# Windowed attention with a gated feed-forward on one core: scores and values as one whole-array product per query block, queries laid with zeros

## The chip, the cores and the metric

The kernel runs on one core of a Trainium2 chip. The metric is the device time of one execution in microseconds (us). The kernel before was timed three times: 671.68, 670.58 and 668.12 us, median 670.58. Inputs and outputs lie in device memory. The host lays the inputs out once, before the launch, and that is not timed.

## What is computed

There are four batches, eight heads, 768 positions and 64 features a head. Each position attends to the keys at a distance under 16, and to 24 summaries: the elementwise maximum of each block of 32 keys, with the mean of the same 32 values. The result of all heads side by side (3072 tokens of 512) goes through a feed-forward of width 2048 with a gate.

```python
k_sum = k.reshape(B, H, nb, 32, D).max(axis=3)
v_sum = v.reshape(B, H, nb, 32, D).mean(axis=3)
mask_l = np.abs(pos[:, None] - pos[None, :]) < 16
scores_l = np.where(mask_l, scale * q @ k.T, -1e9)
scores_s = scale * q @ k_sum.T + np.log(32)
a = softmax(concatenate([scores_l, scores_s]))
x = a @ concatenate([v, v_sum])
h = x @ w_in
g = np.where(h >= 1, h, np.where(h <= -1, 0.0, (h + 1) ** 2 / 4))
out = g @ w_out
```

## The kernel before

**Tiling.** A chunk is half a batch: 384 positions, six query blocks of 64. There are eight chunks (c), and in each four pairs of heads (p). A query block sees 96 neighbouring keys and 24 summaries, 120 columns. The partitions of a pair's tiles hold the 64 features of its first head, then those of its second.

**Attention of one pair.** Steps are named by a letter, chunk and pair; the letters are those of the table `steps` in the code. r, k, q, y and v load raw keys, windowed keys, queries, raw values and windowed values. R reduces raw keys to their maxima (DVE, tile ks), C copies them behind the windowed keys (POOL). Y, Z, V and W do the same for values, through a transpose on PE (tile vs_ps). S are the scores: for each of six blocks and each head one product of 64 features by 64 queries by 120 keys, into two tiles of PSUM (s_ps, one for each head). The two blocks of a step t go to partitions 0 to 63 and 64 to 127. M scales and masks (DVE, tile e) and finds the maxima (den). E is exp with its sum on ACT, D the reciprocal on DVE, N the norm on POOL. T transposes the weights on PE (t_ps), P copies them out of PSUM (ACT, tile pt). A are the values: for each block and head one product with 64 columns of v held and 64 columns of pt streamed, all into one PSUM tile o_ps. X copies o_ps to a rounded high part (ACT, xhi), and L subtracts it to get the low part (DVE, xlo).

**Feed-forward.** A chunk runs 16 steps f. F is the first product (tile h, 12 products of 384 columns: four head pairs, three of high and low parts each). G, H, I and J are the gate on ACT and DVE, O its low part on POOL. B is the second product, two steps behind F, into three PSUM tiles acc that live for the whole chunk (9 products of 512 columns). U and o copy a chunk's result out and store it. The weights are fetched (w) and split into high and low parts (a to e, on ACT, DVE and POOL) once, during chunk 0.

**Order.** The text OPENING lists chunk 0, and the attention of chunk 1, step by step for all engines. After it, the loop at the end of the function fixes the order on PE alone, and a scheduler places the work of the other engines and the DMA issues on SP's queue. In the loop, f = 0, 4, 8 and 12 of chunk c first run `meet`: the values of one pair of the next chunk (at f = 0: the fourth pair of this chunk), then at once the scores of the pair after it. f = 3, 7, 11 and 15 run `turn`: transposes of that pair, ahead of B.

**Buffers.** Six PSUM tiles are shared by scores, transposes, values and acc (pool `ps`), two are for h. Queries have four buffers (Q_BUFS), windowed keys three, windowed values two. Raw keys, raw values and results share three. Queries lie in device memory as blocks of 128 rows (both heads' features) by 128 columns, each head's 64 queries in its own half of the columns and zeros in the other half. Chunk 0 loads whole blocks; later chunks load the two parts that are not zero.

Of the kernel before, what the change touches and what calls it, by code (L numbers as in the profile page):

```python
# [19 lines left out]
P = 128  # L20
# [3 lines left out]
QB = 64  # L24
# [13 lines left out]
Q_BUFS = 4  # L38
# [10 lines left out]
F060 F061 F062 F063 F052 F053 J03 O03 B03 J04 O04 B04 e6 q12 q13 w9 wa wb wc a9 aa wd we wf c7 d7 e7 c8 d8 b9 ba bb  # L49
# [5 lines left out]
W11 V10 W10 S10 B0e M10 E101 D101 N101 E100 D100 N100 B0f U02 U00 S11 M11 E111 E110 S12 o02 U01 o01 T101 P101 D111  # L55
# [5 lines left out]
         [("kraw", 3), ("vraw", 3)], [("v", 2), ("v", 3)], [("q", 0), ("q", 1)]]  # L61
K_COPY = "vgvg"
# [4 lines left out]
def fused_kernel(ctx: ExitStack, tc: tile.TileContext, q2, kT, kwin, vT, vwin, w_in, w_out, mask, ident, out):  # L67
# [12 lines left out]
    mask_sb = const.tile([P, NT + 1, KA], F32, name="mask_sb")  # L80
# [94 lines left out]
    def load_queries(c, p):  # L175
        b, hf = divmod(c, NHALF)
        blocks = q2[b, p, :, hf * NB:(hf + 1) * NB, :]
        halves_of = [slice(j * D, (j + 1) * D) for j in range(2)]
        if c == 0:
            q_t = at_first["q", p]  # L180
            nc.sync.dma_start(out=q_t, in_=blocks)
            q_ts[c, p] = [q_t[rows, :, rows] for rows in halves_of]
        else:

            q_t = input_tile(load, "q", [P, NB, QB], c, p)
            for rows in halves_of:
                nc.sync.dma_start(out=q_t[rows], in_=blocks[rows, :, rows])
            q_ts[c, p] = [q_t[rows] for rows in halves_of]
# [43 lines left out]
    def scores(c, p):  # L232


        q_t, k_t = q_ts[c, p], k_ts[c, p]
        s_ps = [ps.tile([P, 512], F32, tag="ps", name=f"s_ps{c}_{p}_{j}") for j in range(2)]
        for t in range(NT):
            for j in range(2):
                rows = slice(j * D, (j + 1) * D)
                for i in range(2):  # L240
                    blk = 2 * t + i
                    nc.tensor.matmul(s_ps[j][i * QB:(i + 1) * QB, t * KA:(t + 1) * KA],  # L242
                                     q_t[j][:, blk], k_t[rows, blk, :], start=True, stop=True)
# [37 lines left out]
    def values(c, p):  # L281
        o_pss[c, p] = ps.tile([P, 512], F32, tag="ps", name=f"o_ps{c}_{p}")
        for blk in range(NB):
            cols = slice(blk * QB, (blk + 1) * QB)
            for j in range(2):
                nc.tensor.matmul(o_pss[c, p][j * D:(j + 1) * D, cols], v_ts[c, p][:KA, blk, j * D:(j + 1) * D],  # L286
                                 pts[c, p, j][:KA, cols], start=True, stop=True)

    def high(c, p):
        hi = xpool.tile([P, T], F32R, tag=f"xhi{p}", name=f"xhi{c}_{p}")  # L290
        lo = xpool.tile([P, T], F32R, tag=f"xlo{p}", name=f"xlo{c}_{p}")
        nc.scalar.copy(out=hi, in_=o_pss[c, p][:, :T])  # L292
        xs[c, p] = (hi, lo)

    def low(c, p):
        hi, lo = xs[c, p]
        nc.vector.tensor_tensor(out=lo, in0=o_pss[c, p][:, :T], in1=hi.bitcast(F32), op=ALU.subtract)  # L297
# [188 lines left out]
```

## Time and profile before

| | us |
|---|---|
| median of three runs | 670.58 |
| the profiled execution, its span | 670.7 |
| PE busy (matmul) | 633.5 |
| PE busy (weight load) | 559.4 |
| ACT busy | 367.5 |
| POOL busy | 267.1 |
| DVE busy | 259.4 |
| mean granted TensorE clock | 0.982 |

The profiler's span runs from the first to the last instruction. PE is matmul, PEld the load of the operand that is held in the array, DVE the vector engine, ACT the scalar engine, POOL the general engine, SP the queue that issues the DMAs. "x12" is a number of instructions, "idle before" the idle time of the engine just before them with what ended it. The ends of matmul records are modelled, so that records which follow each other overlap by the time that the array takes to drain; starts are what to read.

### The profile page before, as it was taken

The numbers are of one execution on the slowest core, as the hardware profiler recorded it, in microseconds if no ns is written. First come the engines' busy times: TensorE is split into PE (matmuls) and PEld (weight loads), VectorE is DVE, ScalarE is ACT, GpSimd is POOL, SyncE is SP. The second block draws the span as 40 slices with busy tenths as digits, with TensorE's granted clock in tenths as the row PEclk, the third lists the DMA queues.
The fourth block names the chain that finished last, engine by engine and source line by source line (L and its number), as shares of the span: only waits on it lengthen the run. The fifth ranks groups of instructions, "written<-read, shape, count | busy, mean of one in ns | idle before, by whom it ended". The sixth has DMA issues, their size and how long they took to land.

```text
span 670.7 us, 11802 instructions
## 1 busy us (share of the span) xinstructions
PE 633.5 (94%) x4448; PEld 559.4 (83%) x4448; DVE 259.4 (39%) x561; ACT 367.5 (55%) x945; POOL 267.1 (40%) x300
## 2 busy tenths in 40 slices
PE   2579998779999999999999999999999999999997
PEld 2478986668888888988888889888888988889996
DVE  5899974642233321245322322336222322311111
ACT  3889745555555545555554554555545645544332
POOL 2589996333332333234333333334233333322221
PEclk9789999879999999999999999999999999999999
DMA  8999703851111401154111311135110200000001
GB/s 285 311 354 323 250 1 85 248 145 52 53 52 53 145 19 35 52 169 124 53 53 48 106 45 52 52 112 181 53 42 11 88 19 19 1 17 32 1 1 47
DMA packets 49768, 63.56 MB, mean 95 GB/s; under 512 B 24880, under 2 KB 33328, under 8 KB 49712
## 3 DMA queue, kind: packets, MB, share of 16 engines
q1 hardware_dynamic: 49712, 62.81, 30.9%
q8 instruction: 35, 0.57, 0.4%
q14 instruction: 21, 0.17, 0.1%
HBM read 56.51 MB, written 6.29 MB: 94 GB/s over the span
## 4 chain that ended last, share of the span: by engine, by line
PE 82%; DMA 7%; ACT 4%; DVE 4%; issue 2%; POOL 1%; SPq 0%; ACTq 0%; DVEq 0%; POOLq 0%
PE h L307 36%; PE acc L338 36%; PE o_ps L286 4%; PE s_ps L242 3%; DMA raw<-in_w_out 3%; PE t_ps L275 3%; DMA raw<-in_w_in 2%; DMA kraw<-in_kT 1%; ACT e L260 1%; DMA first<-in_vT 1%; DMA first<-in_kT 1%; ACT raw L110 1%; DVE c L124 1%; DVE w L130 1%; DVE c L127 1%
## 5 line engine op out<-in xcount | busy, mean ns | idle before, releaser
L307 PE MATMUL h<-xhi,halves 128*128 128x384 f32 x1024 | 285.4, 341 | 5.6 <-DVE t L319 5.5
L338 PE MATMUL acc<-halves,ghi 128*128 128x512 f32 x768 | 240.2, 394 | 0.0
L329 POOL TENSOR_TENSOR glo<-t,ghi 128x384 fp32r<-128x384 f32 x128 | 129.3, 1013 | 200.6 <-ACT ghi L324 194.5
L307 PEld LDWEIGHTS h<-xhi,halves 128*128 128x128 f32 x1024 | 188.5, 189 | 14.1 <-DVE t L319 4.8
L319 DVE SCALAR_TENSOR_TENSOR t<-h,t 128x384 f32<-128x384 f32 x128 | 70.8, 557 | 280.7 <-ACT t L316 268.9
L307 PE MATMUL h<-xlo,halves 128*128 128x384 f32 x512 | 173.3, 338 | 0.0
L338 PEld LDWEIGHTS acc<-halves,ghi 128*128 128x128 f32 x768 | 145.1, 189 | 27.9
L338 PE MATMUL acc<-halves,glo 128*128 128x512 f32 x384 | 154.2, 401 | 0.0
L313 ACT ACTIVATE t<-h,ones_half 128x384 f32<-128x384 f32 x128 | 73.6, 578 | 130.5 <-PE h L307 120.0
L260 ACT ACTIVATE e<-e,den 128x120 f32<-128x120 f32 x192 | 73.3, 383 | 63.8 <-DVE den L255 63.8
L324 ACT CAST ghi<-t 128x384 fp32r<-128x384 f32 x128 | 65.3, 513 | 64.5 <-DVE t L319 64.0
L307 PEld LDWEIGHTS h<-xlo,halves 128*128 128x128 f32 x512 | 96.8, 189 | 4.3 <-DVE xlo L297 0.4
L338 PEld LDWEIGHTS acc<-halves,glo 128*128 128x128 f32 x384 | 72.5, 189 | 12.3 <-issue 1.0
L270 POOL TENSOR_TENSOR e<-e,den 128x360 f32<-128x360 f32 x64 | 49.8, 790 | 61.6 <-DVE den L266 55.8
L316 ACT ACTIVATE t<-t 128x384 f32<-128x384 f32 x128 | 66.8, 525 | 3.7
L214 POOL COPY k<-ks 128x144 f32<-128x144 f32 x30 | 9.2, 310 | 86.4 <-DMA k<-in_kwin 61.1
L143 POOL TENSOR_TENSOR halves<-w,halves 128x1024 fp32r<-128x1024 f32 x16 | 38.6, 2415 | 0.9
L230 POOL COPY v<-v 24x640 f32<-24x640 f32 x30 | 21.5, 717 | 39.7 <-issue 37.2
L286 PEld LDWEIGHTS o_ps<-pt,v 120*64 120x64 f32 x720 | 25.0, 144 | 13.8 <-ACT ghi L324 7.5
L297 DVE TENSOR_TENSOR xlo<-o_ps,xhi 128x384 fp32r<-128x384 f32 x32 | 17.7, 554 | 47.3 <-ACT xhi L292 47.3
L260 ACT ACTIVATION_READ_ACCUMULATOR e<-e,den 128x1 f32 x192 | 35.9, 187 | 0.0
L275 PE MATMUL t_ps<-ident_sb,e 128*120 128x128 f32 x192 | 30.8, 298 | 5.2 <-POOL e L270 5.0
(56 smaller groups left out, 426.4 us busy)
## 6 DMA issues: line engine op xcount, KB each, us to landing
k<-in_kwin SPq DMA_DIRECT2D x28, 360.0 KB, 4.3
v<-in_vwin SPq DMA_DIRECT2D x30, 288.0 KB, 3.1
raw<-in_w_in SPq DMA_DIRECT2D x16, 512.0 KB, 10.8
raw<-in_w_out SPq DMA_DIRECT2D x16, 512.0 KB, 11.0
out<-o SPq DMA_DIRECT2D x24, 256.0 KB, 2.1
q<-in_q SPq DMA_DIRECT2D x56, 96.0 KB, 4.0
kraw<-in_kT SPq DMA_DIRECT2D x13, 384.0 KB, 3.8
vraw<-in_vT SPq DMA_DIRECT2D x13, 384.0 KB, 3.8
```

The lines of the kernel that those rows point to most:

```text
L143: nc.gpsimd.tensor_tensor(out=lo, in0=converting[i].bitcast(F32), in1=hi.bitcast(F32), op=ALU.subtract)
L260: nc.scalar.activation(out=e[:, t, :], in_=e[:, t, :], func=AF.Exp, bias=nm[:, t:t + 1], scale=1.0, accum_out=den[:, t:t + 1])
L270: nc.gpsimd.tensor_tensor(out=e, in0=e, in1=den.unsqueeze(2).broadcast_to([P, NT, KA]), op=ALU.mult)
L275: nc.tensor.transpose(t_pss[c, p, j][:KA, t * P:(t + 1) * P], es[c, p, j][:, t, :], ident_sb)
L286: nc.tensor.matmul(o_pss[c, p][j * D:(j + 1) * D, cols], v_ts[c, p][:KA, blk, j * D:(j + 1) * D], pts[c, p, j][:KA, cols], start=True, sto ...
L307: nc.tensor.matmul(hs[c, f][:, :T], weight["win", f][w][:, k * P:(k + 1) * P], x, start=(k == 0 and n == 0), stop=(k == NK - 1 and n == 2))
L313: nc.scalar.activation(out=ts[c, f], in_=hs[c, f][:, :T], func=AF.Relu, bias=ones_half, scale=0.5)
L316: nc.scalar.square(out=ts[c, f], in_=ts[c, f])
L319: nc.vector.scalar_tensor_tensor(out=ts[c, f], in0=hs[c, f][:, :T], scalar=1.0, in1=ts[c, f], op0=ALU.max, op1=ALU.min)
L324: nc.scalar.copy(out=hi, in_=ts[c, f])
L329: nc.gpsimd.tensor_tensor(out=lo, in0=ts[c, f], in1=hi.bitcast(F32), op=ALU.subtract)
L338: nc.tensor.matmul(acc[c][i], a[:, rows], weight["wout", f][w], start=(f == 0 and n == 0), stop=(f == NF - 1 and n == 2))
```

## The change

- **Queries** are loaded as whole blocks, zeros included, in every chunk: one DMA of 384 KB for a pair in place of two of 96 KB. Q_BUFS goes from 4 to 2. In OPENING the loads of queries 2 and 3 of chunk 1 (q12, q13) move to behind the scores S10 and S11.
- **Scores**: one product per block for both heads, 128 rows by 128 held columns by 120 streamed ones; the zeros keep the heads apart. A row of s_ps is now a query of the first head (0 to 63) or of the second, and the two tiles hold blocks 0 to 2 and 3 to 5. The mask tile has five positions instead of four, loaded by one DMA, and the second tile uses them one further on.
- **Values**, from chunk 2 on: one product per block with all 128 columns of v held and 128 columns of pt streamed, into two PSUM tiles of three blocks. Half of the results (one head's weights with the other head's values) is not used. X and L read the used quarters: four instructions of 64 partitions by 192 columns each, in place of one of 128 by 384. Chunks 0 and 1 (`QUARTERED`) keep twelve products into one tile.
- **Order in the loop**: `meet` is split. Scores stay ahead of F; values follow F of the same step (at f = 0 they stay first).

```diff
-Q_BUFS = 4
+Q_BUFS = 2
+QUARTERED = (0, 1)
...
-    mask_sb = const.tile([P, NT + 1, KA], F32, name="mask_sb")
+    mask_sb = const.tile([P, 2 * NT - 1, KA], F32, name="mask_sb")
...
-            q_t = input_tile(load, "q", [P, NB, QB], c, p)
-            for rows in halves_of:
-                nc.sync.dma_start(out=q_t[rows], in_=blocks[rows, :, rows])
-            q_ts[c, p] = [q_t[rows] for rows in halves_of]
+        q_ts[c, p] = input_tile(load, "q", [P, NB, P], c, p)
+        nc.sync.dma_start(out=q_ts[c, p], in_=q2[b, p, :, hf * NB:(hf + 1) * NB, :])
...
-        for t in range(NT):
-            for j in range(2):
-                rows = slice(j * D, (j + 1) * D)
-                for i in range(2):
-                    blk = 2 * t + i
-                    nc.tensor.matmul(s_ps[j][i * QB:(i + 1) * QB, t * KA:(t + 1) * KA],
-                                     q_t[j][:, blk], k_t[rows, blk, :], start=True, stop=True)
+        for blk in range(NB):
+            j, t = divmod(blk, NT)
+            nc.tensor.matmul(s_ps[j][:, t * KA:(t + 1) * KA], q_ts[c, p][:, blk, :], k_ts[c, p][:, blk, :], start=True, stop=True)
...
+            for g in range(2):
+                o_ps = ps.tile([P, 512], F32, tag="ps", name=f"o_ps{c}_{p}_{g}")
+                for t in range(NT):
+                    cols = slice(t * P, (t + 1) * P)
+                    nc.tensor.matmul(o_ps[:, cols], v_t[:KA, g * NT + t, :], pts[c, p, g][:KA, cols], start=True, stop=True)
+                for j in range(2):
+                    rows = slice(j * D, (j + 1) * D)
+                    own = o_ps[rows, :T].rearrange("p (t h q) -> p t h q", h=2, q=QB)[:, :, j, :]
+                    o_pss[c, p].append((rows, slice(g * NT * QB, (g + 1) * NT * QB), own))
...
-        nc.scalar.copy(out=hi, in_=o_pss[c, p][:, :T])
+        for rows, cols, o in o_pss[c, p]:
+            nc.scalar.copy(out=hi[rows, cols] if c in QUARTERED else shaped(hi[rows, cols]), in_=o)
...
-        nc.vector.tensor_tensor(out=lo, in0=o_pss[c, p][:, :T], in1=hi.bitcast(F32), op=ALU.subtract)
+        for rows, cols, o in o_pss[c, p]:
+            hi, lo = (x[rows, cols] if c in QUARTERED else shaped(x[rows, cols]) for x in xs[c, p])
+            nc.vector.tensor_tensor(out=lo, in0=o, in1=hi.bitcast(F32), op=ALU.subtract)
...
-                if f % 4 == 0:
-                    meet(c, NPAIR - 1) if f == 0 else meet(c + 1, f // 4 - 1)
-                    if f == 0:
-                        do(f"B{c - 1}{NF - LAG:x}")
+                pair, at = divmod(f, NF // NPAIR)
+                if f == 0:
+                    valued(c, NPAIR - 1)
+                    do(f"B{c - 1}{NF - LAG:x}")
+                if at == 0:
+                    scored(c + 1, pair)
                 s = f"{c}{f:x}"
                 do(f"F{s}0 F{s}1 F{s}2 F{s}3 G{s} H{s} I{s} J{s} O{s}")
-                if f % 4 == 3 and c + 1 < NCH:
-                    turn(c + 1, f // 4)
+                if at == 0 and pair:
+                    valued(c + 1, pair - 1)
+                if at == 3 and c + 1 < NCH:
+                    turn(c + 1, pair)
```

On PE, in chunk 2 at f = 4, these rows stood behind the acc products of f = 1. The digits behind a name are chunk and pair (and head or half), the last number a running one; "x2" is two products in a row.

```order
L338 MATMUL acc2_2_2422<-halves2_557,ghi2_1_2395 128x512 x2
L286 MATMUL o_ps3_0_2484<-pt3_0_0_2461,v3_0_2328 64x64
L286 MATMUL o_ps3_0_2484<-pt3_0_1_2467,v3_0_2328 64x64
L242 MATMUL s_ps3_1_0_2501<-k3_1_2469,q3_1_2471 64x120 x2
L242 MATMUL s_ps3_1_1_2502<-k3_1_2469,q3_1_2471 64x120 x2
L307 MATMUL h2_4_2537<-xhi2_0_1685,halves3_564 128x384
```

The two o_ps rows stand six times in turn, the two s_ps rows three times. In the same place of the changed program:

```order
L341 MATMUL acc2_2_2338<-halves2_532,ghi2_1_2311 128x512 x2
L227 MATMUL s_ps3_1_0_2399<-k3_1_2385,q3_1_2387 128x120 x3
L227 MATMUL s_ps3_1_1_2400<-k3_1_2385,q3_1_2387 128x120 x3
L310 MATMUL h2_4_2429<-xhi2_0_1674,halves3_539 128x384
L310 MATMUL h2_4_2429<-xhi2_3_2206,halves3_539 128x384
L281 MATMUL o_ps3_0_0_2450<-pt3_0_0_2377,v3_0_2253 128x128 x3
L281 MATMUL o_ps3_0_1_2454<-pt3_0_1_2383,v3_0_2253 128x128 x3
L341 MATMUL acc2_0_2336<-halves3_539,glo2_2_2333 128x512
```

Of the twelve h products between scores and values the first and the last are shown. Twelve and twelve products became six and six, and the values moved behind h.

On DVE, where chunk 1 takes over from chunk 0, the reciprocals of chunk 1's third and fourth pair (den1_2, den1_3) stood among the reductions of batch 2's raw keys and values (ks2, vs2):

```order
L265 TENSOR_SCALAR den1_2_1_1326<-den1_2_1_1326 128x3
L218 TENSOR_REDUCE vs2_0_1559<-vraw2_0_1555 128x24
L266 RECIPROCAL den1_2_1_1326<-den1_2_1_1326 128x3
L265 TENSOR_SCALAR den1_3_0_1381<-den1_3_0_1381 128x3
L211 TENSOR_REDUCE ks2_1_1660<-kraw2_1_1653 128x24
L266 RECIPROCAL den1_3_0_1381<-den1_3_0_1381 128x3
L266 RECIPROCAL den1_3_1_1383<-den1_3_1_1383 128x3
```

Now:

```order
L249 TENSOR_SCALAR den1_2_1_1279<-den1_2_1_1279 128x3
L202 TENSOR_REDUCE ks2_0_1464<-kraw2_0_1458 128x24
L250 RECIPROCAL den1_2_1_1279<-den1_2_1_1279 128x3
L249 TENSOR_SCALAR den1_3_0_1328<-den1_3_0_1328 128x3
L209 TENSOR_REDUCE vs2_0_1499<-vraw2_0_1495 128x24
L250 RECIPROCAL den1_3_0_1328<-den1_3_0_1328 128x3
L250 RECIPROCAL den1_3_1_1330<-den1_3_1_1330 128x3
L202 TENSOR_REDUCE ks2_1_1599<-kraw2_1_1593 128x24
```

The reduction of the second pair's keys (ks2_1) moved behind the last reciprocals; that of the third pair moved behind the masks of chunk 2's first scores, ahead of the gates that follow.

On SP's queue, the loads between the last weights of chunk 0 and the first raw keys of batch 2 stood so:

```order
L173 DMA k1_3_1183<-in_kwin 128x720
L187 DMA q2_0_1515<-in_q2 64x6x64 x2
L350 DMA out<-o0_2_1251 128x512
L173 DMA k2_0_1513<-in_kwin 128x720
L187 DMA q2_1_1657<-in_q2 64x6x64
L167 DMA kraw2_0_1511<-in_kT 128x768
```

Now:

```order
L174 DMA k1_3_1150<-in_kwin 128x720
L179 DMA q1_2_1174<-in_q2 128x768
L179 DMA q1_3_1226<-in_q2 128x768
L353 DMA out<-o0_2_1214 128x512
L174 DMA k2_0_1460<-in_kwin 128x720
L353 DMA out<-o0_1_1251 128x512
L353 DMA out<-o0_0_1216 128x512
L168 DMA kraw2_0_1458<-in_kT 128x768
L188 DMA v1_2_1342<-in_vwin 96x768
```

Two query loads of chunk 1 stand ahead of the first result's store, and the queries of chunk 2 moved behind the raw keys.

More of the change, by code (lines that the diff above doesn't have):

```diff
@@ L48 @@
 c4 d4 e4 b6 b7 b8 I02 J02 F040 F041 F042 F043 O02 B02 a7 a8 c5 c6 d5 e5 d6 q10 q11 G03 H03 I03 F050 F051 G04 H04 I04
-F060 F061 F062 F063 F052 F053 J03 O03 B03 J04 O04 B04 e6 q12 q13 w9 wa wb wc a9 aa wd we wf c7 d7 e7 c8 d8 b9 ba bb
+F060 F061 F062 F063 F052 F053 J03 O03 B03 J04 O04 B04 e6 w9 wa wb wc a9 aa wd we wf c7 d7 e7 c8 d8 b9 ba bb
 G05 G06 H06 I06 F070 F071 F072 F073 H05 I05 J05 F080 J06 O05 F081 F082 F083 O06 B05 G07 H07 e8 c9 d9 I07 J07 O07 F090
@@ L54 @@
 O0d B0d k10 k11 k12 v10 v11 bf cf df ef G0e H0e I0e G0f H0f I0f J0e J0f O0e O0f k13 C10 C11 C12 C13 Z10 Z11 V11 Z12
-W11 V10 W10 S10 B0e M10 E101 D101 N101 E100 D100 N100 B0f U02 U00 S11 M11 E111 E110 S12 o02 U01 o01 T101 P101 D111
+W11 V10 W10 S10 q12 B0e M10 E101 D101 N101 E100 D100 N100 B0f U02 U00 S11 q13 M11 E111 E110 S12 o02 U01 o01 T101 P101 D111
 N111 o00 D110 N110 T100 P100 M12 S13 E120 D120 N120 A10 X10 L10 T111 P111 T110 P110 M13 E121 D121 N121 F100 v12 V12
@@ L176, in load_queries @@
         b, hf = divmod(c, NHALF)
[L177 to L183, printed above, removed]
-            q_t = input_tile(load, "q", [P, NB, QB], c, p)
-            for rows in halves_of:
-                nc.sync.dma_start(out=q_t[rows], in_=blocks[rows, :, rows])
-            q_ts[c, p] = [q_t[rows] for rows in halves_of]
+        q_ts[c, p] = input_tile(load, "q", [P, NB, P], c, p)
+        nc.sync.dma_start(out=q_ts[c, p], in_=q2[b, p, :, hf * NB:(hf + 1) * NB, :])
     def load_raw_vals(c, p):
@@ L281, in values, with shaped @@
     def values(c, p):
[L282 to L287, printed above, removed]
+        v_t = v_ts[c, p]
+        if c in QUARTERED:
+            o_ps = ps.tile([P, 512], F32, tag="ps", name=f"o_ps{c}_{p}")
+            for blk in range(NB):
+                g, t = divmod(blk, NT)
+                for j in range(2):
+                    nc.tensor.matmul(o_ps[j * D:(j + 1) * D, blk * QB:(blk + 1) * QB], v_t[:KA, blk, j * D:(j + 1) * D],
+                                     pts[c, p, g][:KA, t * P + j * D:t * P + (j + 1) * D], start=True, stop=True)
+            o_pss[c, p] = [(slice(0, P), slice(0, T), o_ps[:, :T])]
+        else:
+            o_pss[c, p] = []
+            for g in range(2):
[3 more added lines that the diff above has]
+                    nc.tensor.matmul(o_ps[:, cols], v_t[:KA, g * NT + t, :], pts[c, p, g][:KA, cols], start=True, stop=True)
+                for j in range(2):
+                    rows = slice(j * D, (j + 1) * D)
+                    own = o_ps[rows, :T].rearrange("p (t h q) -> p t h q", h=2, q=QB)[:, :, j, :]
+                    o_pss[c, p].append((rows, slice(g * NT * QB, (g + 1) * NT * QB), own))
+    def shaped(ap):
+        return ap.rearrange("p (t q) -> p t q", q=QB)
     def high(c, p):
@@ L353, in load_constants @@
     def load_constants():
-        for i in range(2):
-            rows = slice(i * QB, (i + 1) * QB)
-            nc.sync.dma_start(out=mask_sb[rows], in_=mask[rows, i:i + NT + 1])
+        nc.sync.dma_start(out=mask_sb, in_=mask)
         nc.sync.dma_start(out=ident_sb, in_=ident)
@@ L380, in heads, with follow, valued, scored @@
                 (f"y{s} " if first else "") + f"v{s} " + (f"Y{s} " if first else ""))
-    def meet(c, p):
+    def follow(c, p):
+        return (c, p + 1) if p + 1 < NPAIR else (c + 1, 0)
+    def valued(c, p):
         if c < NCH:
             do(f"A{c}{p} X{c}{p} L{c}{p}")
-        c, p = (c, p + 1) if p + 1 < NPAIR else (c + 1, 0)
+    def scored(c, p):
         if c < NCH:
-            before, scored, valued = heads(c, p)
-            do(before + " " + scored + " " + valued)
+            do(" ".join(heads(c, p)))
     def turn(c, p):
@@ L394, in turn @@
         do(f"Z{s} V{s} W{s} T{s}0 P{s}0 T{s}1 P{s}1")
-        c, p = (c, p + 1) if p + 1 < NPAIR else (c + 1, 0)
+        c, p = follow(c, p)
         if c < NCH:
```

4 lines of the change are left out of this document (1 added, 3 removed).

## The prediction

> **What bounds the kernel now.** The page first: how full TensorE (PE) is, over the span and in 40 slices of it, and the chain that ended last.
>
> ```profile
> PE 633.5 (94%) x4448; PEld 559.4 (83%) x4448; DVE 259.4 (39%) x561; ACT 367.5 (55%) x945; POOL 267.1 (40%) x300
> PE   2579998779999999999999999999999999999997
> PE 82%; DMA 7%; ACT 4%; DVE 4%; issue 2%; POOL 1%; SPq 0%; ACTq 0%; DVEq 0%; POOLq 0%
> ```
>
> PE carries 82% of the chain. Next the windows, to see whether it ever rests in the steady part:
>
> ```profile
> 150.00:250.00 100.00, 100.00 (x754) 88.60 (x753) 29.63 (x70) 54.17 (x148) 34.46 (x42) 1.00 0.21 60
> 450.00:550.00 100.00, 100.00 (x718) 89.32 (x717) 33.10 (x73) 53.81 (x146) 34.97 (x44) 1.00 0.24 74
> ```
>
> The columns are PE, weight load (PEld), DVE, ACT, POOL, clock, DMA share. From 150 on PE is never without an instruction and at full clock; ACT is half idle, DVE two thirds. There, time added to or taken from PE goes one to one into the end. A full PE may still drain between shapes, so I read its timeline in one place where values and scores stand together (start, length from first start to last end):
>
> ```profile
> 302.86 0.33 PE L307 MATMUL h<-xhi,halves 128*128 128x384 f32 x1
> 303.03 0.27 PE L222 MATMUL vs_ps<-ident_sb,vs 128*24 128x128 f32 x1
> 303.14 0.82 PE L275 MATMUL t_ps<-ident_sb,e 128*120 128x128 f32 x6
> ...
> 304.02 0.62 PE L338 MATMUL acc<-halves,ghi 128*128 128x512 f32 x2
> ...
> 305.17 0.39 PE L338 MATMUL acc<-halves,glo 128*128 128x512 f32 x1
> 305.40 0.62 PE L338 MATMUL acc<-halves,ghi 128*128 128x512 f32 x2
> 305.95 0.92 PE L286 MATMUL o_ps<-pt,v 120*64 120x64 f32 x24
> 306.80 0.85 PE L242 MATMUL s_ps<-k,q 64*64 64x120 f32 x24
> 307.57 0.45 PE L307 MATMUL h<-xhi,halves 128*128 128x384 f32 x1
> 307.86 0.34 PE L307 MATMUL h<-xlo,halves 128*128 128x384 f32 x1
> 308.03 0.51 PE L307 MATMUL h<-xhi,halves 128*128 128x384 f32 x2
> ```
>
> A 512-column product starts 0.23 after the one before it (305.17, 305.40), a 384-column one 0.17 (307.86, 308.03). The last acc product thus starts at 305.63 and has streamed by 305.86. The first h product counts as starting one step ahead of the second, at 307.69. **Values and scores together cost 307.69 − 305.86 = 1.83**: values 0.85 (to about 306.70), scores 0.98.
>
> **What runs at once inside.** Twelve products stand as 24 records: two records to a product. A narrow window of the scores shows their beat:
>
> ```profile
> 307.16 0.49 PE L242 MATMUL s_ps<-k,q 64*64 64x120 f32 x12
> ...
> L242 PE MATMUL s_ps<-k,q x672: 262/263/314, 106.7 to 577.0; 64*64 64x120 f32 x168
> L286 PE MATMUL o_ps<-pt,v x720: 222/222/370, 20.0 to 595.7; 120*64 120x64 f32 x180
> ```
>
> The twelve, 0.26 each, start within 0.49 − 0.26 = 0.23. That is three groups of four, about 0.10 apart: four quarter-array records (64 rows by 64 columns) stream their 120 columns at the same time. Six groups are 0.62; the other 0.36 of the 0.98 goes at the two edges of the burst. Values: the last of 24 starts 0.92 − 0.22 = 0.70 after the first, 11 steps of 0.06 for pairs of half-array records.
>
> **The change on PE.** Six products use the whole array instead of twelve that share it: 12 records that cannot share. No row has a full-array fp32 product of this kind. Its nearest row in streaming is the transpose: six start within 0.82 − 0.27 = 0.55, a step of 0.11 for 128 columns; a score group gives 0.10 for 120. The other limit is the weight load, now 128 columns instead of 64:
>
> ```profile
> 303.69 0.19 PEld L338 LDWEIGHTS acc<-halves,glo 128*128 128x128 f32 x1
> ...
> 307.57 0.19 PEld L307 LDWEIGHTS h<-xhi,halves 128*128 128x128 f32 x1 [0.16 <-issue]
> 307.68 0.19 PEld L307 LDWEIGHTS h<-xlo,halves 128*128 128x128 f32 x1
> ```
>
> The load of 303.69 lets its acc product begin in effect at 304.02 − 0.23 = 303.79, and that of 307.57 its h product at 307.69: 0.10 to 0.12 from load to stream. Load and stream give the same 0.11, so I take **0.11 a record**. Below, 0.10 (scores all stream, load hidden); above, 0.19, if no load ran beside a stream.
>
> The Trainium skill, "TensorE: Matmul & The Clock Gate", section "LDWEIGHTS (loading the stationary operand)", has the load go with its columns, P / 1.2 ns. By it 128 columns are 107 ns, above the 0.10 of the scores' stream, so twelve score records would be 1.28 rather than 1.23. The row of 303.69 bears that out.
>
> Values: 12 × 0.11 = 1.32, against 0.85: +0.47. Scores: 1.32 against 0.98: +0.34. The edges go: vs_ps after h (302.86, 303.03) keeps the plain step of 0.17, so full-array products of other types follow without a drain. The sum is +0.81 where both stand together. That is 23 places: three in chunk 1's loop, four in each of chunks 2 to 6; the last values, in chunk 7, stand alone:
>
> ```profile
> 594.40 0.62 PE L338 MATMUL acc<-halves,ghi 128*128 128x512 f32 x2
> 594.96 0.92 PE L286 MATMUL o_ps<-pt,v 120*64 120x64 f32 x24
> 595.80 0.50 PE L338 MATMUL acc<-halves,glo 128*128 128x512 f32 x1
> 596.14 0.63 PE L338 MATMUL acc<-halves,ghi 128*128 128x512 f32 x2
> ```
>
> These cost 596.14 − 0.23 − 594.86 = 1.05, now 1.32: +0.27. **Steady part: 23 × 0.81 + 0.27 = 18.9.** At 0.10 a score record it is 16.1.
>
> **The copies out of PSUM.** One copy and one subtraction per pair become four each, of 64x192, from chunk 2 on.
>
> ```profile
> L292 ACT CAST xhi<-o_ps 128x384 fp32r<-128x384 f32 x32 | 15.2, 477 | 25.2 <-PE o_ps L286 25.0
> L226 ACT ACTIVATE v<-vs_ps 24x128 f32<-24x128 f32 x30 | 7.8, 264 | 2.5 <-PE vs_ps L222 1.8
> L297 DVE TENSOR_TENSOR xlo<-o_ps,xhi 128x384 fp32r<-128x384 f32 x32 | 17.7, 554 | 47.3 <-ACT xhi L292 47.3
> ```
>
> A 192-column copy lies between 0.26 and 0.48; I take 0.33, and 0.36 for the subtraction: +0.8 on ACT and +0.9 on DVE in 19 us, on engines with 45% and two thirds free. Only the fourth pair is needed soon: its values stand at the head of a chunk, and h wants it after one acc step (2.07), the scores (1.32) and nine h products (1.56), 4.9 later. Four copies and the last subtraction take about 1.8, at most 2.6. Cost nothing; if that cover were gone, six chunks would pay what is late. Exps and gates behind the extra copies on ACT are late by under 1 us, and their products two h steps away (over 4 us).
>
> **The opening.** The four score bursts of chunk 0 run at the low clock:
>
> ```profile
> 9.57 1.48 PE L242 MATMUL s_ps<-k,first 64*64 64x120 f32 x24 [9.57 <-POOL first L214]
> 36.84 1.54 PE L275 MATMUL t_ps<-ident_sb,e 128*120 128x128 f32 x6
> 25.25 1.10 ACT L110 ACTIVATE raw<-raw 128x1024 f32<-128x1024 f32 x1 [1.17 <-DMA raw<-in_w_in]
> 17.04 0.42 PE L222 MATMUL vs_ps<-ident_sb,vs 128*24 128x128 f32 x1
> 40.56 11.42 SPq L187 DMA_DIRECT2D q<-in_q  x8
> 48.00:106.00 58.00, 57.77 (x289) 51.24 (x287) 49.06 (x85) 42.63 (x64) 57.36 (x40) 1.00 0.57 175
> ```
>
> Transposes there step by 0.22 (1.54 less the 0.42 of one, over five), so a burst is 12 × 0.22 = 2.6 instead of about 1.3: +1.3 four times, 5.2. The first values stand behind all four, and ACT copies them ahead of its first weight (L110), for which it waits 1.17. Above, 5.2 − 1.17 = 4.0 reaches the weight conversions, which then keep POOL full; below, nothing. I take **+1.1**, nearer to nothing, because the second and third slice have PE busy 5 and 7 tenths: the bursts slide into gaps.
>
> The queries of chunk 1: eight loads held the queue for 11.42; now two whole-block loads go there and two later, so at most those 11 us go. But from 48 to 106 POOL is busy for 57.36 of 58.00 and PE for 57.77: earlier weights find both full. I take 0; if DMA were the limit there, it would be up to −11.
>
> **From chunk 0 to chunk 1** (106 to 140) PE waits:
>
> ```profile
> 126.55 0.54 PE L275 MATMUL t_ps<-ident_sb,e 128*120 128x128 f32 x3 [2.50 <-POOL e L270]
> 130.27 0.55 PE L275 MATMUL t_ps<-ident_sb,e 128*120 128x128 f32 x3 [1.15 <-POOL e L270]
> 139.72 0.69 PE L307 MATMUL h<-xhi,halves 128*128 128x384 f32 x1 [3.94 <-DVE t L319]
> ...
> 128.09 0.95 DVE L211 TENSOR_REDUCE ks<-kraw 128x24 f32<-128x768 f32 x1 [1.57 <-DMA kraw<-in_kT]
> ...
> k<-in_kwin SPq DMA_DIRECT2D x28, 360.0 KB, 4.3
> ```
>
> Five score bursts here (chunk 1's four, chunk 2's first) add 5 × 0.34 = 1.7. Two stalls may shrink: the key reduction of the next batch no longer stands ahead of the last reciprocals on DVE. What is late next is the 3.94: on DVE the third pair's key reduction now stands ahead of the gates that free h, its load behind v on the SP queue, which waits for the fourth pair's values. With two query buffers the third pair's queries of chunk 1 load only after its first scores, some 5 us ahead of their use, about what the landing of such a load takes (4.3 for 360 KB); out, kraw and vraw are queued behind them. In sum 0, between −4 and +4.
>
> **Sum.** 670.7 (the profiled span, the median of the runs to 0.1) + 18.9 + 1.1 + 0 = **690.7**.
>
> **Rivals.**
> *Faster: each record has a fixed price.* 48 records in 1.83 are 0.038 each; with 24 fewer the place costs 0.92: 23 × −0.9 = −21, **650**. It decides below 1.83 / 24 = 0.076 a record. For it: the averages 0.035 and 0.041 of the two bursts are near each other. Against it: four records start inside one 0.10 beat, and transposes step by 0.11. 3%.
> The Trainium skill, "TensorEngine Tiling", section "Instruction Overhead", states about 60 cycles of overhead for each matmul. If that were the price here, halving the records would pay as in this rival; the groups of four speak against it.
> *Loads don't hide behind full-array fp32 streams:* 0.19 a record, 2.3 a burst, 23 × 2.7 + 1.2 = 63: **735**. The transposes' step of 0.11 speaks against it. 4%.
> *A new PSUM wait:* values now take two slots, of three beside acc, while two hold scores; the second frees when DVE's mask has read. The mask has twelve h products (12 × 0.17 = 2.1) for it; a reduction of 0.95 in its way in the twelve pairs that load new keys is 12 × 0.95 = 11: **702**. 8%.
> *The waits of the transition go:* 2.50, 1.15 and 3.94 are 7.6, less the 1.7 of the scores' growth that they hid: **685**; with the loads of the opening on the path as well, **675**. 4%.
>
> **How the numbers follow.** 80% for the forecast, 1% for no measurable change by something not listed. 684 to 699 comes from the bounds (−2.8 for the stream and −4; +4, +3 and 1 for a wait now and then); it leaves out the two far rivals, the PSUM wait and the 675. A measurement tells about 0.5% (3.4 us) from no change: faster by over 0.5% 3%, within it 1%, slower 96%.
>
> **What would show it.** s_ps and o_ps at six products (12 records) each, starting 0.11 apart, 1.3 a burst; the period of four f steps grows from 19.2 to 20.0; no PE wait from 150 to 600; q gone from 40 to 52. I am wrong if the records start under 0.08 or over 0.13 apart, if PE waits for DVE ahead of the second half of o_ps, or if chunk 2 begins more than 5 us from where it did.

## The result and the profile after

The changed kernel takes 689.92 us (median of 4 runs, 688.76 to 692.42); the kernel before, on the same chip, 671.13 (668.12 to 673.95). The ratio is 1.0285, interval [1.0245, 1.0325]: slower. The profiled execution spans 688.4 us, against 670.7. The forecast was 690.7, from 684 to 699.

The page first: the line of busy times, PE's 40 slices, and the shares of the chain that ended last.

```profile
PE 653.2 (95%) x3776; PEld 594.7 (86%) x3776; DVE 285.0 (41%) x633; ACT 381.9 (55%) x1017; POOL 267.8 (39%) x300
PE   4489998789999999999999999999999999999997
PE 88%; ACT 3%; DVE 2%; DMA 2%; issue 2%; POOL 1%; SPq 0%; POOLq 0%; DVEq 0%; ACTq 0%
```

PE has 672 instructions fewer and is busy 19.7 us longer (653.2 against 633.5). The windows in the steady part (PE, weight load, DVE, ACT, POOL, clock, DMA share, GB/s):

```profile
150.00:250.00 100.00, 100.00 (x575) 92.10 (x574) 33.80 (x83) 54.45 (x157) 32.84 (x40) 1.00 0.21 70
450.00:550.00 100.00, 100.00 (x572) 92.01 (x572) 38.20 (x88) 55.41 (x158) 33.78 (x42) 1.00 0.28 93
```

PE still never rests. The number of its records in 100 us fell from 754 and 718 to 575 and 572. They are longer in their place, and nobody keeps them waiting. The place in which scores and values stand, in PE's timeline:

```profile
310.97 0.62 PE L341 MATMUL acc<-halves,ghi 128*128 128x512 f32 x2
311.42 1.49 PE L227 MATMUL s_ps<-k,q 128*128 128x120 f32 x12
312.68 0.44 PE L310 MATMUL h<-xhi,halves 128*128 128x384 f32 x1
312.95 0.34 PE L310 MATMUL h<-xlo,halves 128*128 128x384 f32 x1
...
314.69 0.34 PE L310 MATMUL h<-xhi,halves 128*128 128x384 f32 x1
314.87 1.50 PE L281 MATMUL o_ps<-pt,v 120*128 120x128 f32 x12
316.13 0.48 PE L341 MATMUL acc<-halves,glo 128*128 128x512 f32 x1
316.45 0.63 PE L341 MATMUL acc<-halves,ghi 128*128 128x512 f32 x2
```

Read as before: the last acc product starts at 311.20 and has streamed by 311.43; the first h product begins in effect at 312.95 − 0.17 = 312.78. Scores cost **1.35**. The last h product has streamed by 314.86, and acc begins in effect at 316.45 − 0.23 = 316.22: values cost **1.36**. One record is 0.275 long by its group,

```profile
L227 PE MATMUL s_ps<-k,q 128*128 128x120 f32 x336 | 42.0, 275 | 2.5 <-DMA q<-in_q 1.8 <-POOL k L205 0.8
L281 PE MATMUL o_ps<-pt,v 120*128 120x128 f32 x288 | 36.1, 275 | 0.0
```

so twelve score records start within 1.49 − 0.275 = 1.215, eleven steps of 0.110. The idle column of the values is 0.0, and from 150 to 620 the list of PE's waits is empty: no wait on a PSUM tile there.

What a place costs on average is read from the period. The first h product of chunk 2 starts at 215.50 and that of chunk 6 at 537.05 (before: 213.44 and 521.71). That is 80.39 a chunk against 77.07, **0.83 more at each of its four places**. A chunk's first h product stands behind the values and the scores of its f = 0. Up to that of chunk 2, four places in all, the change has cost 2.06.

The first chunk, in PE's timeline, and what PE waited for over the whole span (us in total, times, longest):

```profile
8.47 5.44 PE L227 MATMUL s_ps<-k,first 128*128 128x120 f32 x24 [8.47 <-DMA first<-in_q]
13.70 1.73 PE L227 MATMUL s_ps<-first 128*128 128x120 f32 x12
...
18.87 1.60 PE L227 MATMUL s_ps<-first 128*128 128x120 f32 x12 [0.95 <-POOL first L205]
...
38.56 0.44 PE L310 MATMUL h<-xhi,halves 128*128 128x384 f32 x1
```

```profile
PE h L310 <- DVE t L322: 6.5, 3, 3.9
...
PE t_ps L259 <- POOL e L254: 4.0, 4, 1.3
...
PE s_ps L227 <- DMA q<-in_q: 1.8, 1, 1.8
```

The first h product of the kernel starts at 38.56, where the kernel before has it at 40.28. The opening did not grow by 1.1; it became 1.7 shorter. That is the one step with the wrong sign. By the first h product of chunk 1 (120.20 against 120.60) 1.3 of the 1.7 is lost again.

### The profile page after: what moved, and what is told of

Its sections match the earlier page's. It is cut to its first block, busy times and chain, and to the rows that moved or that the text cites. A ratio compares the mean times of both kernels' runs of the same rounds, so it can differ in the third digit from the quotient of the medians.

```text
span 688.4 us, 10599 instructions
## 1 busy us (share of the span) xinstructions
PE 653.2 (95%) x3776; PEld 594.7 (86%) x3776; DVE 285.0 (41%) x633; ACT 381.9 (55%) x1017; POOL 267.8 (39%) x300
## 4 chain that ended last, share of the span: by engine, by line
PE 88%; ACT 3%; DVE 2%; DMA 2%; issue 2%; POOL 1%; SPq 0%; POOLq 0%; DVEq 0%; ACTq 0%
PE h L310 37%; PE acc L341 37%; PE s_ps L227 6%; PE o_ps L281 5%; PE t_ps L259 3%; ACT e L244 1%; DMA first<-in_q 1%; DMA vraw<-in_vT 1%; ACT raw L111 1%; ACT raw L116 1%; PE o_ps L272 1%; POOL glo L332 1%; DMA q<-in_q 1%; PE vs_ps L213 0%; DVE c L125 0%
## 5 line engine op out<-in xcount | busy, mean ns | idle before, releaser
L234 DVE SCALAR_TENSOR_TENSOR e<-s_ps,mask_sb 128x360 f32<-128x360 f32 x64 | 33.3, 527 | 36.0 <-PE s_ps L227 35.8
L227 PEld LDWEIGHTS s_ps<-k,q 128*128 128x128 f32 x336 | 41.8, 193 | 5.0 <-DVE den L250 2.0
L300 DVE TENSOR_TENSOR xlo<-o_ps,xhi 64x192 fp32r<-64x192 f32 (+1 forms) x104 | 38.3, 368 | 17.3 <-ACT xhi L294 16.2
L227 PE MATMUL s_ps<-k,q 128*128 128x120 f32 x336 | 42.0, 275 | 2.5 <-DMA q<-in_q 1.8
L294 ACT CAST xhi<-o_ps 64x192 fp32r<-64x192 f32 (+1 forms) x104 | 33.7, 324 | 9.6 <-PE o_ps L281 4.9
L281 PEld LDWEIGHTS o_ps<-pt,v 120*128 120x128 f32 x288 | 35.7, 192 | 0.5
```

Of the source, the lines that this page charges most:

```text
L227: nc.tensor.matmul(s_ps[j][:, t * KA:(t + 1) * KA], q_ts[c, p][:, blk, :], k_ts[c, p][:, blk, :], start=True, stop=True)
L281: nc.tensor.matmul(o_ps[:, cols], v_t[:KA, g * NT + t, :], pts[c, p, g][:KA, cols], start=True, stop=True)
```

## The experiments

Each run stands beside runs of the kernel before on the same chip. "Period" is the length of a chunk in the profiled execution (first h product of chunk 2 to that of chunk 6, by four), "first h" the start of the kernel's first h product.

| run | median us | before | ratio, interval | period | first h |
|---|---|---|---|---|---|
| before | | 671.13 | | 77.07 | 40.28 |
| after | 689.92 | 671.13 | 1.0285 [1.0245, 1.0325] | 80.39 | 38.56 |
| e1_values_shared | 684.12 | 672.07 | 1.0182 [1.0157, 1.0206] | 79.23 | 38.10 |
| e2_values_whole_alone | 708.76 | 672.07 | 1.0534 [1.0506, 1.0562] | 84.24 | 41.18 |
| e3_order_and_loads | 676.14 | 672.07 | 1.0060 [1.0039, 1.0081] | 77.80 | 40.75 |
| e4_mask_in_one_load | 671.81 | 672.07 | 0.9995 [0.9979, 1.0012] | 77.07 | 39.83 |
| e5_shifted_tiles | 671.82 | 672.53 | 0.9989 [0.9974, 1.0004] | 77.07 | 41.20 |
| e6_scores_two_at_once | 696.45 | 672.53 | 1.0357 [1.0339, 1.0375] | 81.39 | 38.71 |
| e7_scores_96_columns | 690.02 | 672.53 | 1.0255 [1.0233, 1.0277] | 80.39 | 37.87 |
| e8_copies_twice | 695.90 | 672.53 | 1.0358 [1.0339, 1.0376] | 81.19 | 38.23 |
| e9_tiles_at_512 | 669.88 | 673.61 | 0.9962 [0.9944, 0.9980] | 77.07 | 38.60 |
| e10_after_tiles_off | 691.28 | 673.61 | 1.0263 [1.0247, 1.0280] | 80.63 | 39.56 |
| e11_before_both | 671.18 | 673.61 | 0.9968 [0.9951, 0.9985] | 77.07 | 38.37 |

### The parts of the 0.83: order, scores, values

The first step from before to after takes the order and the loads alone.

```diff
-Q_BUFS = 4
+Q_BUFS = 2
...
-                nc.sync.dma_start(out=q_t[rows], in_=blocks[rows, :, rows])
+        nc.sync.dma_start(out=q_t, in_=q2[b, p, :, hf * NB:(hf + 1) * NB, :])
+        q_ts[c, p] = [q_t[j * D:(j + 1) * D, :, j * D:(j + 1) * D] for j in range(2)]
...
+                if at == 0 and pair:
+                    valued(c + 1, pair - 1)
```

> The kernel before with only the order of after (table of the opening, values behind h) and whole-block loads of the queries in two buffers; every product, copy and the mask as before. Theory (switching between shapes of the array costs PE at each edge, so bursts that stand apart pay twice): values alone 1.05 for 0.85, scores 0.98 or some 0.1 to 0.2 more, 23 x 0.2 to 0.4 = 5 to 9, so 675 to 680, and first h of chunk 0 within 0.5 of 40.3. Rival (order and loads are free in the steady part): 669 to 671; then all of the growth of after lies in the whole-array products.

```profile
305.62 0.62 PE L329 MATMUL acc<-halves,ghi 128*128 128x512 f32 x2
306.18 0.85 PE L233 MATMUL s_ps<-k,q 64*64 64x120 f32 x24
306.95 0.44 PE L298 MATMUL h<-xhi,halves 128*128 128x384 f32 x1
307.23 0.34 PE L298 MATMUL h<-xlo,halves 128*128 128x384 f32 x1
...
308.96 0.34 PE L298 MATMUL h<-xhi,halves 128*128 128x384 f32 x1
309.23 0.92 PE L277 MATMUL o_ps<-pt,v 120*64 120x64 f32 x24
310.08 0.50 PE L329 MATMUL acc<-halves,glo 128*128 128x512 f32 x1
310.42 0.63 PE L329 MATMUL acc<-halves,ghi 128*128 128x512 f32 x2
```

In PE's timeline of this run scores cost 307.06 − 306.08 = 0.98 as before, but values, alone between h and acc, cost 310.19 − 309.13 = 1.06 where they cost 0.85 beside the scores. The same records in another order take 0.2 more, because each burst now has two edges to full-array products. By the period it is (77.80 − 77.07) / 4 = 0.18 a place. Order and loads by themselves make the kernel 0.6% slower. The Trainium skill, "TensorEngine Tiling (Array Packing)", section "Key Properties", says that a change of the tiling mode drains TensorE; the 0.2 of this run agrees with it, though the trace shows the time and not the drain.

The second step makes the scores whole too, and leaves the values shared.

```diff
-QUARTERED = (0, 1)
+QUARTERED = tuple(range(NCH))
```

> The kernel after with its values as twelve half-array products in every chunk (scores whole, order and loads as after). Theory (time of PE goes by what shares the array at once): scores stay at 1.3 a burst; values alone between h and acc cost 1.05, as the last values of the kernel before did, against 1.35 whole; 24 bursts x 0.30 = 7 less than after, about 682 to 684. Rival (each record has a price of its own, 0.04): values at 24 records cost more than at 12, so 690 or above. Rival (the growth comes from the copies out of PSUM, which are single again here): 671 to 675.

It came out at 684.1, at the upper end of what was expected. From e3 to e1 the period grows by 79.23 − 77.80 = 1.43, 0.36 a place: whole scores. From e1 to after it grows by 1.16, 0.29 a place: whole values. **0.18 + 0.36 + 0.29 = 0.83.** The three are differences of the same four periods, so that they add up is no test of its own; what tests them is that they agree with the costs read in place (1.06 for 0.85, 1.35 for 0.98, 1.36 for 1.06). The copies of e1 are single again, so they have no part in its 0.36 and 0.18. The 0.29 holds the four copies of after together with its whole values; e8 below looks at them.

### Values whole, in the old order

```diff
+                    nc.tensor.matmul(o_ps[:, t * P:(t + 1) * P], v_ts[c, p][:KA, blk, :],
+                                     pts[c, p][:KA, :, blk * QB:(blk + 1) * QB], start=True, stop=True)
```

> The kernel before with only the values of chunks 2 to 7 as six whole-array products, two PSUM tiles and four copies; scores, queries, mask and order as before. Theory: values 1.32 against 0.85, 23 x 0.47 + 0.27 = 11.1, so 682; if the scores now pay an entry of their own that the values paid for both (0.1 to 0.2), up to 686. Rival (a wait on the second PSUM tile or on the copies, since here scores stand right behind values): PE waits for ACT or DVE in the trace, 23 x 0.5 or more on top, 693 or above.

It is the slowest of all. PE's timeline at two places, and the windows of the second:

```profile
297.47 1.50 PE L297 MATMUL o_ps<-pt,v 120*128 120x128 f32 x12
298.90 0.42 PE L242 MATMUL s_ps<-k,q 64*64 64x120 f32 x4
299.83 0.83 PE L242 MATMUL s_ps<-k,q 64*64 64x120 f32 x20 [0.51 <-issue]
...
322.18 0.83 PE L242 MATMUL s_ps<-k,q 64*64 64x120 f32 x20 [2.17 <-issue]
322.94 0.44 PE L327 MATMUL h<-xhi,halves 128*128 128x384 f32 x1
323.23 0.47 PE L327 MATMUL h<-xlo,halves 128*128 128x384 f32 x1
323.50 0.84 PE L327 MATMUL h<-xhi,halves 128*128 128x384 f32 x2
```

```profile
317.00:320.00 3.00, 3.00 (x22) 2.44 (x20) 1.99 (x3) 1.78 (x5) 1.33 (x3) 1.00 0.73 245
320.00:323.00 3.00, 0.82 (x22) 0.69 (x21) 2.78 (x7) 0.62 (x2) 0.81 (x2) 1.00 0.37 101
323.00:326.00 3.00, 3.00 (x11) 3.00 (x11) 2.07 (x6) 1.68 (x9) 0.00 (x0) 0.55 0.59 160
```

The four records into the first score tile start, then PE stands still: 0.51 at 21 of 23 places, 1.60 and 2.17 at the other two. The profile names no releaser ("issue"). By the pools it is the second score tile: three acc tiles, two of values and one of scores fill the six, so the seventh waits for a tile of values to be copied out. The run with doubled copies, below, shows that releaser by name, and here DVE's timeline around the wait of 2.17 fits it:

```profile
319.43 0.95 DVE L211 TENSOR_REDUCE ks<-kraw 128x24 f32<-128x768 f32 x1 [0.53 <-DMA kraw<-in_kT]
...
320.50 0.95 DVE L218 TENSOR_REDUCE vs<-vraw 128x24 f32<-128x768 f32 x1
321.37 1.47 DVE L317 TENSOR_TENSOR xlo<-o_ps,xhi 64x192 fp32r<-64x192 f32 x4
```

Two reductions stand ahead of the subtractions, the first two of which free the first tile of values. PE goes on 0.10 after the end of one of these subtractions, here and at the places with the short wait alike. That is a PSUM wait like the third rival's, with its reduction in the way at the two long ones, but at a place that the prediction did not look at: not values behind scores, but scores behind values. In after the twelve h products stand between, and the wait does not occur.

The longer waits cost more than their length. After the 2.17 the granted clock is 0.50 from 323.3 to 326.7 (0.55 in the third window above, which begins earlier), and h products step by 0.32 (323.50 to 324.13 for two) where 0.17 is usual. After the 1.60 it is 0.50 again, from 490.5 to 493.9; the waits of 0.51 had nothing of the kind behind them.

### Is it the record, the load or the stream?

```diff
-            nc.tensor.matmul(s_ps[j][:, t * KA:(t + 1) * KA], q_ts[c, p][:, blk, :], k_ts[c, p][:, blk, :], start=True, stop=True)
+            for h in range(2):
+                rows = slice(h * D, (h + 1) * D)
+                nc.tensor.matmul(s_ps[j][rows, t * KA:(t + 1) * KA], q_ts[c, p][rows, blk, rows], k_ts[c, p][rows, blk, :], start=True, stop=True)
```

> The kernel after with each whole-array score product as two quarter-array products on the two diagonal quarters (64 rows by 64 columns each), without the zeros: 24 records, two at once. Theory (time goes by what shares the array at once): twelve beats of 0.10 plus edges of 0.25 to 0.36, 1.45 to 1.56 a burst against 1.35, 2 to 5 above after, 692 to 695. Rival (a price per record of 0.04): 0.98 a burst, 681. Rival (each record takes the array for itself, 0.11): 2.6 a burst, 720.

PE's timeline and its group of score records:

```profile
312.09 1.45 PE L229 MATMUL s_ps<-k,q 64*64 64x120 f32 x24
```

```profile
L229 PE MATMUL s_ps<-k,q 64*64 64x120 f32 x672 | 40.5, 267 | 2.4 <-DMA q<-in_q 1.6 <-POOL k L205 0.8
```

24 records start within 1.45 − 0.27 = 1.18, 0.10 for two. The kernel before had 0.10 for four of the same records, after has 0.11 for one. The place is (81.39 − 80.39) / 4 = 0.25 dearer than in after, which makes 1.60 a burst: twelve beats of 0.10 and the full 0.36 of edges, a little above the expected 1.56, as 696.5 is above 695. A price for each record is out in both forms, 681 and 720.

```diff
-            nc.tensor.matmul(s_ps[j][:, t * KA:(t + 1) * KA], q_ts[c, p][:, blk, :], k_ts[c, p][:, blk, :], start=True, stop=True)
+            n = KA if t == NT - 1 else KW
+            nc.tensor.matmul(s_ps[j][:, t * KW:t * KW + n], q_ts[c, p][:, blk, :], k_ts[c, p][:, blk, :n], start=True, stop=True)
```

> The kernel after with four of the six score products of a pair streaming 96 columns instead of 120: the scores on the summary keys of those four blocks are left out (the mask reads columns of the next block in their place). Theory (the weight load of 128 columns sets the step): records still start 0.11 apart, 1.35 a burst, 688 to 690. Rival (the stream sets it): eight of twelve records start 0.08 to 0.09 apart, 0.2 less a burst, 24 x 0.2 = 5 less, 684 to 686.

```profile
312.48 1.49 PE L228 MATMUL s_ps<-k,q 128*128 128x96 f32 x12
```

Twelve records, eight of them with 96 columns, take 1.49 from the first start to the last end, as with 120 in after, and the period is 80.39 in both. So the step of 0.11 is not the stream's. The weight loads of the same bursts, in after and in this run, take the same time too:

```profile
311.19 1.53 PEld L227 LDWEIGHTS s_ps<-k,q 128*128 128x128 f32 x12
312.26 1.53 PEld L228 LDWEIGHTS s_ps<-k,q 128*128 128x128 f32 x12
```

One load is 0.19 long, so the twelve start within 1.34 in both. What is left as the cause is the load of 128 columns; no run changed the number of held columns of a full-array record, so this is by elimination. The Trainium skill, "TensorE: Matmul & The Clock Gate", section "LDWEIGHTS (loading the stationary operand)", by which the prediction had put the loads above the streams, agrees with the 0.11.

### Are the copies hidden?

```diff
-            nc.scalar.copy(out=hi[rows, cols] if c in QUARTERED else shaped(hi[rows, cols]), in_=o)
+            for _ in range(1 if c in QUARTERED else 2):
+                nc.scalar.copy(out=hi[rows, cols] if c in QUARTERED else shaped(hi[rows, cols]), in_=o)
```

(and the subtraction alike)

> The kernel after with every copy of values out of PSUM into x, high and low part, made twice from chunk 2 on (+1.3 on ACT and +1.4 on DVE at each pair). Theory (the copies are hidden: values of three pairs are wanted a chunk's rest later, those of the fourth 4.9 after they end): the period of four f steps stays 20.1, no wait of PE on xhi or xlo over 0.5 at a chunk's head, 689 to 691. Rival (they are at the edge of their cover): PE waits 1 to 1.5 at the head of each of six chunks, 696 to 699.

The theory's 689 to 691 did not hold. 695.9 is near the rival's time, but not by the rival's wait. At the head of chunk 4, PE's timeline:

```profile
377.08 0.82 PE L227 MATMUL s_ps<-k,q 128*128 128x120 f32 x6
378.27 0.90 PE L227 MATMUL s_ps<-k,q 128*128 128x120 f32 x6 [0.36 <-DVE xlo L302]
```

h does not wait for x. The second score tile waits for DVE's subtraction, the last reader of the values' PSUM tile: the wait of e2 again, at the one place of a chunk where values still stand ahead of scores. The first h product of that chunk starts 0.6 later behind the values than in after; 0.2 more is lost before the second score burst, and the later three places cost the same as in after. So the single copies do cost nothing (in after the records step by 0.11 from one score tile to the next at every place of the steady part), but the cover that the prediction named for the fourth pair (4.9 until h wants it) was the wrong one: the score tile wants its slot sooner.

### The opening

The mask in one load, on the kernel before (its two halves lie side by side in memory beforehand):

```diff
-        for i in range(2):
-            rows = slice(i * QB, (i + 1) * QB)
-            nc.sync.dma_start(out=mask_sb[rows], in_=mask[rows, i:i + NT + 1])
+        nc.sync.dma_start(out=mask_sb, in_=mask)
```

> The kernel before with its mask laid ready and loaded by one DMA where two stood. Theory (the opening of after is earlier because the mask takes the queue once, 0.43 where two took 1.18, and raw keys, raw values and first weights follow earlier): first weights on the queue at about 12.8 or earlier where before had 13.57, first h of chunk 0 at 38.8 to 39.6 where before had 40.28, and the end 0.5 to 1.5 earlier. Rival (the gain of the opening is from something else): first weights and first h as before, within 0.3.

The first weights stand on the queue at 12.46 instead of 13.57, and the first h product comes at 39.83, 0.45 earlier: less than expected, no more than the kernels with the old place differ among themselves (40.28 to 41.20), and no difference in the time. It does not reach 38.56.

After's mask tile is also 480 bytes longer in each partition, which moves every load tile behind it. First 32 bytes more on the kernel before:

```diff
-    ones_half = const.tile([P, 1], F32, name="ones_half")
+    ones_half = const.tile([P, 9], F32, name="ones_half")[:, :1]
```

> The kernel before with one constant tile 32 bytes longer, so that every load tile behind it lies at a multiple of 64 bytes (before: 32 beyond one; after: at one, since its mask is 480 bytes longer). Theory (the tiles' place sets how fast the loads of the opening land): packets of 1024 bytes of the weights between 15 and 40 us take 0.047 us each as in after, where before had 0.053; they land earlier, first h of chunk 0 0.8 to 1.5 earlier than the 40.3 to 41.2 of the kernels with the old place, and the end as much earlier, 669.5 to 671. Rival (the loads go faster in after because PE fetches and reads less beside them): packets stay at 0.052 to 0.054, first h and time as before.

No effect: first h at 41.20. A place at a multiple of 64 bytes is not it. Then as far as in after, the same 32 bytes on the kernel after, and mask and place together on the kernel before:

```diff
-    ones_half = const.tile([P, 1], F32, name="ones_half")
+    ones_half = const.tile([P, P], F32, name="ones_half")[:, :1]
```

> The kernel before with one constant tile 508 bytes longer, so that the load tiles lie where they do in after (the first at byte 19456 of each partition, a multiple of 512; before 18976, and in the run with 32 bytes more 19008, neither a multiple of 128). Theory (the place of the tiles, in steps of 128 bytes or more, sets the speed of the loads): packets of 1024 bytes in the first 70 us take 0.046 to 0.047 us and those of 4096 bytes 0.165 to 0.17, as in after, where before had 0.051 and 0.182; first h of chunk 0 at 38.5 to 39.8 where kernels with the old place had 40.3 to 41.2; the end some 1 us earlier. Rival (something else of after makes its loads faster: its products, its order, its mask): packets stay at 0.050 to 0.052 and 0.18, first h at 40.3 or later.

> The kernel after with one constant tile 32 bytes longer, so that its load tiles lie 32 bytes beyond a multiple of 512. Theory (place of the tiles): packets of 1024 bytes take 0.050 to 0.052 us, of 4096 bytes 0.18, first h of chunk 0 at 39.5 to 41 where after had 38.6, and the end 0.5 to 2 later than after. Rival: packets stay at 0.046 and first h within 0.6 of 38.6.

> The kernel before with its mask in one load and its load tiles at a multiple of 512 bytes, no product changed. Theory (both make the opening earlier, mask 0.5 to 0.9 and place 1 to 1.5): first h of chunk 0 at 38 to 39, end 1 to 2 earlier than before, 669 to 671, within 0.3% of it. Rival (the wait of h on a gate at the head of chunk 1 takes it back): first h of chunk 0 earlier but that of chunk 2 within 0.5 of 213.4, time as before.

The weights land between 15 and 40 us. The window from 15 to 40, with DMA share and GB/s as its last two columns, of the kernel before:

```profile
15.00:40.00 25.00, 14.69 (x150) 11.36 (x147) 21.13 (x49) 20.43 (x61) 16.75 (x21) 0.73 1.06 325
```

of e5, 32 bytes further:

```profile
15.00:40.00 25.00, 13.68 (x126) 10.17 (x126) 20.20 (x45) 19.46 (x60) 15.71 (x21) 0.74 1.06 303
```

of e9, with the tiles where after has them:

```profile
15.00:40.00 25.00, 16.03 (x156) 12.57 (x155) 21.71 (x47) 20.75 (x56) 16.30 (x21) 0.73 1.05 370
```

of after:

```profile
15.00:40.00 25.00, 14.41 (x148) 11.39 (x148) 22.22 (x50) 21.20 (x62) 16.99 (x21) 0.73 1.05 355
```

and of e10, after with its tiles 32 bytes off:

```profile
15.00:40.00 25.00, 13.53 (x139) 10.50 (x138) 21.52 (x49) 20.98 (x63) 16.95 (x21) 0.74 1.06 321
```

The DMA engines are full in all five, and move 355 and 370 GB/s where the load tiles start at a multiple of 512 bytes, 303 to 325 where they don't. In the trace, packets of 1024 bytes in the first 70 us take 0.046 us on average in after and 0.047 in e9, but 0.050 in e10, 0.051 in before and 0.052 in e5; the other eight runs fall in line, 0.046 to 0.047 with after's place and 0.051 with before's. The first h product follows: 38.56 and 38.60 against 40.28 and 41.20, and 39.56 in e10, which still has the one mask load. The Trainium skill, "DMA: Bandwidth & Descriptors", section "How a descriptor splits into AXI transactions", has a descriptor that does not start at a multiple of 256 bytes pay for bytes that are fetched and not used. It speaks of what is read; here the place that is written to was moved. With that difference the five windows agree with it: 19456 (after, e9) is such a multiple, and 18976 (before), 19008 (e5) and 19488 (e10) are not. No run here parts 256 from 512, or 128 from either.

e11 has both edits and its first h product at 38.37, nearly that of after (38.56), whose score bursts are longer. The kernels with after's place and whole scores reach from 37.87 to 38.56 (e7, e8, e1, after), so no cost of the longer bursts is seen in the opening.

e9 leaves every product as it was and only moves the tiles: 669.88 against 673.61, ratio 0.9962 [0.9944, 0.9980]. **It is faster than the kernel before too**, by some 0.4%, for 508 bytes of padding. e11 gives 0.9968 [0.9951, 0.9985]: the single mask load adds nothing that can be measured. The reverse, e10, is not shown in the time: 1.0263 against before, where after has 1.0285, with overlapping intervals.

The earlier opening is only part of that 0.4%, and it is not always kept. In e9's profiled execution, its fastest, the first h product of chunk 2 comes at 208.95, 4.5 earlier than before, though the opening gave 1.7. In e11's, its slowest, it comes at 213.12, only 0.3 earlier, as that run's rival had it. The granted clock from 100 to 150 differs (0.93 in e9, 0.86 in e11, 0.90 before). What decides this was not taken apart.

e10 has one more difference that stays open: its period is 0.24 longer than after's (80.63 against 80.39). In three of a chunk's four groups of f steps, twelve h products start within 1.94 (the first twelve of a group aside), in after in one of the four; elsewhere within 1.91. So the parts of the 0.83 are good to some 0.06.

## Why the prediction was right, step by step

- **PE sets the time from 150 on:** right. Busy 100.00 of 100.00 in both windows, and no wait of PE between 150 and 620 in the trace.
- **0.11 a record:** right. 0.110 to 0.112, and by e7 it is not the stream that sets it, so the lower bound of 0.10 (16.1 for the steady part) is out. A burst is 1.35 rather than 1.32.
- **+0.47 for values, +0.34 for scores:** right in both and for more reasons than were given. By the runs values are 0.18 (the parting from the scores) and 0.29 (the whole products), together 0.47; scores 0.36. "The edges go" was half the story: the shared bursts stood together, and the new order alone, with every product shared, already costs 0.18 by parting them.
- **Copies at no cost:** right; e8 shows the nearest limit in another place than named.
- **The new PSUM wait:** rightly left aside for after, and by e2 the order is why. With whole values in the old place, and scores still shared, the kernel takes 709.
- **The opening, +1.1, "below, nothing":** wrong in sign. The step took all four bursts at 2.6, and gave the rest of the opening no way to gain. Two bursts did take 2.7 each (5.44 together), the next two 1.73 and 1.60, and all of it slid into gaps. The diff's longer mask tile moved the load tiles to a place where the weights land faster, and one load less stood ahead of them; neither was priced. First h is 1.7 earlier; e9 gives the same with the place alone. That the query loads leave the queue (2.48 from 38.27 in place of 11.42) was rightly put at nothing: the first h of chunk 1 is only 0.4 earlier.
- **From chunk 0 to chunk 1, 0:** about right. The waits on POOL of 2.50 and 1.15 became 1.33 and 1.31, the 3.94 stayed at 3.9. Where scores had waited 1.75 for a copy of ACT, they now wait 1.8 for a load of queries, the one that the prediction held to be just long enough. The first h of chunk 2 starts 2.06 later, where the forecast's terms up to there (1.1, 0 and four places of 0.81) make 4.3. The opening is 2.8 better than forecast and the stretch behind it 0.5 worse; these waits were not taken apart.
- **The sum:** 690.7 forecast on the footing of the span, 688.4 in the profiled execution, 689.9 as the median. All of the 2.3 between the two spans stood already at the first h of chunk 2: from there to the end the change costs 15.6, and the terms (19 places of 0.81 and 0.27) make 15.7. That the median comes so near the forecast is in part luck. Each time lies some 2.0 above the span of its own execution (690.43 for 688.4), which a sum put on a span leaves out, and the 2.3 of the early part nearly makes up for it. A growth of 20.0 was forecast; it is 17.7 by the spans and 18.8 by the medians.

The rivals: the fixed price (650) falls by e6, the loads that do not hide (735) by the step of 0.11, the transition's waits that go (685, 675; the second comes to 674 by its own terms) by the 3.9 that stays.

## What to carry to other kernels

Before putting small products together into one that fills the array, read from the trace how many of them start within one beat: four quarter-array records in 0.10 were cheaper than one full-array record of 0.11, zeros and all. Bursts of shared products want to stand next to each other, since parting two of them cost 0.2 here; but a burst that takes more PSUM tiles wants distance to the next that needs them. And when a change makes a constant tile longer, look where the load tiles behind it come to lie.

## What the runs showed of the hardware that was not expected

- The place of a tile in the partition sets the speed of the loads into it: 355 to 370 GB/s at a multiple of 512 bytes, 303 to 325 at 32 or 64 bytes beyond one, with the DMA engines full in both (1024-byte packets 0.046 to 0.047 us against 0.050 to 0.052, in all thirteen runs).
- A full-array fp32 record with 128 columns held steps by 0.11 whether it streams 96, 120 or 128 columns.
- After waits of 2.17 and 1.60 in the midst of a full PE its pace was halved for 3.4 us (granted clock 0.50, h products 0.32 apart instead of 0.17), which is 1.7 us more; the 21 waits of 0.51 did not do this.
- In the opening the granted clock in the windows reads 1.00 from 8 to 24 us, while full-array score records start 0.22 apart from 8.47 on and 0.13 from 13.70 on (5.44 for 24, 1.73 for 12): that column does not show the slow beginning. The trace's first record of the clock begins at 14.2.
